# Attention with a learned distance bias, then a softplus feed-forward: round 1's scores moved into the bias stage, relus moved to ScalarE, rounds 0 and 1 reordered

## The chip, the core and the metric

The kernel runs on one core of one Trainium2 chip. The metric is the device time of one execution in microseconds (us). Three executions of the kernel before took 728.38, 728.56 and 729.88 us; their median is 728.56.

A core has five engines that run side by side and wait for one another on semaphores. TensorE (PE in the rows) does matmuls and transposes and writes to PSUM. VectorE (DVE) and ScalarE (ACT) do elementwise work on SBUF and PSUM. GpSimd (POOL) does elementwise work on SBUF, and SyncE (SP) issues DMAs. Each engine executes its own queue strictly in order.

## The reference

```
scores = (q @ k.T) / sqrt(D)                              B, H, S, D = 4, 8, 576, 64
x      = log1p(|i - j|) / log1p(max(i, 1))                for every pair of positions
bias   = relu(x * w1 + b1) @ w2                           32 hidden units, one output per head
attn   = softmax(scores + bias)
y      = attn @ v                                          -> (2304, 512)
h      = y @ w_in                                          512 -> 2048
out    = softplus(h) @ w_out                               2048 -> 512, float32
```

The bias depends on the position pair and the head, not on the batch.

## The kernel before, in words

**Bias stage.** 36 steps, one per 16 rows of positions. Step s needs four hidden tiles (relu of a scaled distance row plus a per-row term, `emit_hid`, 18 widths between 304 and 576 columns): the first three are always made by VectorE, the fourth by ScalarE for the steps in `RELU_ACT` and by VectorE for the others. TensorE contracts the 32 hidden units (`emit_mm`, into the PSUM tile `acc`, two banks, three buffers in the pool `pb`). `emit_rows` copies `acc` to the SBUF tile `e` in two pieces, nearly always on ScalarE (`EVAC_DVE` gives two of the 72 pieces to VectorE), and SyncE writes `e` to `e_d` in DRAM. The hidden tiles are made `LEAD` = 5 steps ahead of the copies. When 8 steps are written, later steps load bias tiles (128 by 576) back from `e_d`: tiles 0 and 5 after step 7, 1 and 6 after step 15, 2 and 7 after step 23. Tiles 3, 8 and 4 come last, and tile 4 needs the last step's rows.

**Splits.** q and k of a round are split into a high and a low part in fp32r (`u_split`), on VectorE in the bias stage for rounds 0 and 1 (`SPLITS` says at which steps), later with the low parts on GpSimd.

**Rounds.** 16 rounds, each one batch and one pair of heads, 9 score tiles of 128 rows. A score tile is four matmuls of 288 columns (eight for tile 4) into the PSUM tile `s`; VectorE then adds the bias and takes the row extreme in one custom instruction (`first` in `u_s`, written to the probabilities' tile `p` in SBUF); ScalarE takes the exponential in place (`second`); TensorE transposes `p`, VectorE or ScalarE copies the transposes from PSUM (`pt`), and TensorE multiplies with v (`o`). GpSimd copies small tails (`tl`).

**Order.** The order in which the queues are filled is written out by hand. In the strings `ROUND0`, `ROUND` and so on, a token names one piece of work: within round n, `Z`, `ZA`, `ZX` are matmuls, bias-and-extreme and exponential of a tile of round n itself, `S`, `A`, `X` the same for round n+1; `T` and `V` are transposes and their copy (`/a` on ScalarE, `/d` on VectorE); `P` the product with v; `Kh`, `Kl`, `Qh`, `Ql` the splits of round n+2; `I`, `R`, `C` the reciprocal sums; `O` the scaled output; `L`, `ZL` the tails. `SEQ0` puts five score tiles of round 0 into steps 21 to 31 of the bias stage, with one PSUM buffer for them (`ps_s`); a second one (`ps_s2`) is opened when the bias stage is over.

**After the rounds** comes the feed-forward part, which the change doesn't touch.

Of the kernel before, what the change touches and what calls it, by code (L numbers as in the profile page):

```python
# [24 lines left out]
EC = S + 15  # L25
# [63 lines left out]
LOADS0 = {8: "k", 14: "q", 44: "v1", 72: "v", 79: "w"}  # L89
# [15 lines left out]
def tile_log_bias_attention__then__softplus_ffn(  # L105
# [41 lines left out]
    ps_s = [pool(es_s, "ps_s", 1, "right", PSUM)]  # L147
# [15 lines left out]
    pb = pool(es_b, "pb", 3, space=PSUM)  # L163
# [185 lines left out]
    def u_s(n, t):  # L349
# [33 lines left out]

        def first():
# [23 lines left out]
        return pe, first, second  # L408
# [182 lines left out]

# [266 lines left out]
    for s in range(36):  # L858
# [18 lines left out]
    ps_s.append(pool(es_s, "ps_s2", 1, "right", PSUM))  # L877
# [73 lines left out]
    for n in range(N + 1):  # L951
# [9 lines left out]
        toks = {0: ROUND0, N - 1: ROUND15, N: ROUND16}.get(n, ROUND).split()  # L961
# [97 lines left out]
```

## Time and profile before

| | us |
|---|---|
| median of three runs | 728.56 |
| the profiled execution, its time | 728.94 |
| the profiled execution, span from first to last instruction | 727.1 |
| busy: PE, DVE, ACT, POOL | 695.6, 525.1, 524.8, 117.7 |
| share of the chain that ended last: PE, DVE, ACT, DMA | 87%, 5%, 3%, 2% |

The span is what the rows cover; the rest of the 728.94 lies around it. Busy time is summed over the whole span, so it hides that the engines' loads differ by stage. A row of the order-of-time view merges neighbouring instructions of one kind: its second number is the time from the first one's start to the last one's end, "x4" their count. Neighbours overlap a little, so the cost of one instruction in a full queue is the distance between starts, which is somewhat less than its duration.

### The profile page before, as it was taken

To read this page: it belongs to the slowest core of one execution; us is meant where nothing else is said; L and a number is where in the kernel's file an instruction comes from. 1 tells how busy PE (TensorE), PEld (TensorE's weight loads), DVE (VectorE), ACT (ScalarE), POOL (GpSimd) and SP (SyncE) were. 2 spreads that over 40 slices of the span, in tenths; PEclk is the share of its full clock that TensorE was granted. 3 is DMA by queue.
4 is the path that set the end of the run, shared out by engine and by line. 5 is a ranking of instruction groups with operands and counts; after the bars stand their busy time and mean duration, and the time that the engine had idled before them with its cause. 6 is when DMAs were issued, how large, how long until landed. Compare 5 with 4: busy or idle time off the path is not lost.

```text
span 727.1 us, 11884 instructions
## 1 busy us (share of the span) xinstructions
PE 695.6 (96%) x4160; PEld 547.1 (75%) x4160; DVE 525.1 (72%) x1109; ACT 524.8 (72%) x1060; POOL 117.7 (16%) x150
## 2 busy tenths in 40 slices
PE   4868999999999999989999999999999999999998
PEld 2224788877888778757888888988888888888886
DVE  7997877887888877667969595678685554656454
ACT  3967778888888887667867686777677665665654
POOL 0000446444554454120000000000000000000000
PEclk9989999999999999999999999999999999999999
DMA  4865686687677652654232030512020220312121
GB/s 135 316 200 207 219 290 208 212 250 241 191 211 218 186 169 81 166 160 160 75 140 93 30 112 4 175 63 83 30 73 15 102 72 1 130 44 81 65 76 41
DMA packets 47452, 96.77 MB, mean 133 GB/s; under 512 B 6928, under 2 KB 8352, under 8 KB 47392
## 3 DMA queue, kind: packets, MB, share of 16 engines
q1 hardware_dynamic: 47036, 95.41, 40.4%
q8 instruction: 33, 0.54, 0.3%
q10 hardware_dynamic: 356, 0.60, 0.3%
q14 instruction: 27, 0.22, 0.1%
HBM read 67.98 MB, written 28.01 MB: 132 GB/s over the span
## 4 chain that ended last, share of the span: by engine, by line
PE 87%; DVE 5%; ACT 3%; DMA 2%; issue 1%; POOL 1%; ACTq 0%; SPq 0%; POOLq 0%; DVEq 0%
PE y L826 28%; PE h L768 27%; PE s L376 11%; PE o L488 10%; PE t L447 8%; DVE m L202 3%; PE acc L215 2%; ACT p L403 1%; PE t L455 1%; DMA r_d<-r 1%; DMA e_d<-e 1%; DVE p L387 1%; ACT e L237 1%; DMA dist<-in_c_dist_dram 1%; ACT pt L341 0%
## 5 line engine op out<-in xcount | busy, mean ns | idle before, releaser
L768 PE MATMUL h<-x,wi 128*128 128x512 f32 (+1 forms) x960 | 216.4, 374 | 2.5 <-ACT wi L739 1.0
L826 PE MATMUL y<-wo,g 128*128 128x512 f32 x864 | 213.1, 394 | 0.0
L768 PEld LDWEIGHTS h<-x,wi 128*128 128x128 f32 x960 | 170.0, 189 | 39.7 <-ACT wi L739 1.4
L826 PEld LDWEIGHTS y<-wo,g 128*128 128x128 f32 x864 | 161.2, 188 | 37.1
L791 DVE SCALAR_TENSOR_TENSOR u<-u,e 128x512 f32<-128x512 f32 (+1 forms) x80 | 51.0, 637 | 110.0 <-ACT l L788 109.9
L376 PE MATMUL s<-kk,qq 128*128 128x288 f32 x640 | 118.2, 314 | 6.6 <-DVE m L387 6.4
L387 DVE CUSTOM_DVE_ANT_0 p<-s,b 128x576 f32<-128x576 f32 x144 | 106.0, 752 | 18.8 <-PE s L376 16.7
L403 ACT ACTIVATE p<-p,m 128x576 f32<-128x576 f32 x144 | 109.7, 765 | 4.1 <-DVE m L387 1.9
L784 ACT ACTIVATE e<-h 128x512 f32<-128x512 f32 (+1 forms) x80 | 44.3, 554 | 83.8 <-PE h L768 83.8
L376 PEld LDWEIGHTS s<-kk,qq 128*128 128x128 f32 x640 | 89.6, 189 | 12.6 <-DVE m L387 10.4
L447 PE MATMUL t<-ident,p 128*128 128x128 f32 x576 | 88.1, 275 | 2.3 <-ACT p L403 0.8
L341 ACT ACTIVATE pt<-t 128x384 f32<-128x384 f32 (+1 forms) x127 | 58.9, 488 | 41.9 <-PE t L447 39.1
L488 PE MATMUL o<-pt,vn 128*64 128x288 f32 (+3 forms) x672 | 84.5, 399 | 0.0
L447 PEld LDWEIGHTS t<-ident,p 128*128 128x128 f32 x576 | 65.8, 140 | 13.3 <-issue 7.0
L488 PEld LDWEIGHTS o<-pt,vn 128*64 128x64 f32 (+1 forms) x672 | 45.4, 136 | 32.5 <-issue 10.0
L798 ACT ACTIVATE g<-l 128x512 fp32r<-128x512 f32 (+1 forms) x80 | 46.8, 585 | 22.3 <-PE y L826 12.6
L343 DVE COPY pt<-t 128x384 f32<-128x384 f32 x97 | 50.3, 532 | 17.1 <-PE t L447 14.4
L215 PE MATMUL acc<-m,coef 128*32 128x512 f32 (+17 forms) x352 | 41.0, 547 | 15.6 <-DVE m L202 10.3
L420 POOL COPY tl<-p 128x128 f32<-128x128 f32 x80 | 26.0, 345 | 172.5 <-ACT p L403 171.5
L800 DVE TENSOR_TENSOR g<-l,g 128x512 fp32r<-128x512 f32 (+1 forms) x80 | 50.3, 629 | 3.8 <-ACT g L798 3.8
L795 DVE TENSOR_TENSOR l<-l,u 128x512 f32<-128x512 f32 (+1 forms) x80 | 50.4, 630 | 0.0
L793 DVE SCALAR_TENSOR_TENSOR l<-h,l 128x512 f32<-128x512 f32 (+1 forms) x80 | 50.4, 630 | 0.0
(55 smaller groups left out, 668.4 us busy)
## 6 DMA issues: line engine op xcount, KB each, us to landing
e_d<-e SPq DMA_DIRECT2D x36, 295.5 KB, 3.2
kn<-in_k_dram SPq DMA_DIRECT2D x16, 576.0 KB, 5.8
b<-e_d SPq DMA_DIRECT2D x32, 288.0 KB, 5.8
r<-in_moe_w_in_dram SPq DMA_DIRECT2D x16, 512.0 KB, 6.0
r<-in_moe_w_out_dram SPq DMA_DIRECT2D x16, 512.0 KB, 4.0
xr<-x_d SPq DMA_DIRECT2D x28, 256.0 KB, 3.4
vn<-in_v_dram SPq DMA_DIRECT2D x16, 320.0 KB, 3.5
qn<-in_q_dram SPq DMA_DIRECT2D x16, 288.0 KB, 5.2
```

Source lines behind the costliest of these rows:

```text
L215: nc.tensor.matmul(acc[32 * g:32 * g + 32, lo:hi], lhsT=coef.rearrange("p o h -> p (o h)"), rhs=hid[s, g][:, lo:hi], start=True, stop=True ...
L341: nc.scalar.activation(dst, src, AF.Copy)
L376: nc.tensor.matmul(ps[:, half, :SH], lhsT=qt[:, c0:c0 + 128], rhs=kt[:, hd, j, half * SH:half * SH + SH], start=(i == 0 and j == 0), stop= ...
L387: nc.vector.tensor_tensor_reduce(prob[n, t].rearrange("p (a c) -> p a c", a=2), st_["ps"][:, :, :SH], bias[pr, t].rearrange("p (a c) -> p ...
L403: nc.scalar.activation(p, p, AF.Exp, bias=st_["m"], scale=-1.0, accum_out=ssum[n][:, t:t + 1],)
L447: nc.tensor.transpose(ps[:, 128 * i:128 * i + 128], prob[n, t][:, 128 * jb:128 * jb + 128], ident,)
L488: nc.tensor.matmul(o[up, half, lo:hi], lhsT=v_n[n][rows, jb, hd], rhs=pt[n, jb][rows, c0:c0 + hi - lo], start=(jb == 0), stop=(jb == 4 and ...
L768: nc.tensor.matmul(ps[:, :nb], lhsT=wi[f][:, a, 128 * c:128 * c + 128], rhs=xs[bi, c][:, x_, :nb], start=(i == 0), stop=(i == 11),)
L791: nc.vector.scalar_tensor_tensor(u, u, -1.0, e, op0=ALU.add, op1=ALU.subtract)
L793: nc.vector.scalar_tensor_tensor(l, ps, 0.0, l, op0=ALU.max, op1=ALU.add)
L795: nc.vector.tensor_tensor(l, l, u, op=ALU.subtract)
L826: nc.tensor.matmul(y, lhsT=g[:, a, 128 * ts:128 * ts + 128], rhs=wo[f][:, w_], start=(first and i == 0), stop=(last and i == 2),)
```

## The change

Round 1's nine score tiles are computed during the bias stage. `raw` copies each from PSUM, without bias, into the place of its probabilities (`p`, SBUF); later `first` reads it there instead of in PSUM. The table `STAGE` replaces `SEQ0`: `21:D00` is round 0's tile 0 at step 21, as before with bias and exponential, and `21:R15` is round 1's tile 5, copied raw. The second PSUM buffer for scores exists from the start, and `acc` has two buffers instead of three. Round 1's split moves from step 12 to step 4. The fourth relu goes to ScalarE for steps 0 to 29 and 32 (31 relus, 22 before), and all 72 copies of `acc` go to ScalarE. `ROUND0` has no `S` tokens any more, and round 1 has an order of its own.

```diff
 ROUND0 = """
-Z7 S1 T20 ZA7 T30 V20/a A1 S6 S0 A6 T40 X1 ZX7 V30/a Z3 A0 V40/a S2 ZA3 A2 T00 Z8 S5 T10 ZX3
-ZA8 X0 ZX8 A5 ZL2 S7 V10/a S3 V00/d T12 T02 X6 V12/a A7 Z4 A3 V02/a ZA4 X7 T32 V32/d L1 ZX4 T22
-S4 I V22/a T01 R Qh1/d V01/a C S8 A4 X2 T11 X4 ZL3 T31 ZL4 P0 V11/d Kh/a Qh0/d L2 Ql0 L4 X5
-V31/d A8 Ql1 Kl X3 X8 L3 T21 V21/d T41 L0 P1 V41/d P2
+Z7 T20 T30 V20/a A1 ZA7 ZX7 V30/a A0 Z3 X1 T40 A6 X0 V40/a Z4 ZA3 A2 Z8 T10 T00 ZX3 ZA8 ZX8 A5
+V00/d ZL2 V10/a T12 T02 X6 V12/a A7 A3 V02/a ZA4 X7 T32 V32/d L1 ZX4 T22 V22/a I T01 R Qh1/d
+V01/a C A4 T11 X2 X4 ZL3 T31 ZL4 P0 Kh/a V11/d X5 Qh0/d L2 Ql0 Kl X3 A8 Ql1 L4 V31/d T21 L0 P1
+X8 L3 V21/d T41 V41/d P2
+"""
+
+ROUND1 = """
+Qh1/d Kh/a P3 P4 T20 Qh0/a I T02 S2 T11 V20/d V02/d V11/a A2 S3 T12 V12/a T00 V00/a S7 A3 O T10
...
 """
-LOADS0 = {8: "k", 14: "q", 44: "v1", 72: "v", 79: "w"}
+LOADS0 = {6: "k", 11: "q", 37: "v1", 63: "v", 70: "w"}
-RELU_ACT = {s for s in range(36) if s % 5 in (0, 2, 4)}
-
-EVAC_DVE = {3, 6}
-SPLITS = (2, 12)
+RELU_ACT = {*range(30), 32}
+
+SPLITS = (2, 4)
-SEQ0 = {21: 0, 24: 5, 26: 1, 29: 6, 31: 2}
+STAGE = """
+21:D00 21:R15 23:R10 24:R16 25:R12 26:D01 26:D05 30:R13 31:R11 31:R17 32:D02 33:D06 33:R18
+34:R14
+"""
-    ps_s = [pool(es_s, "ps_s", 1, "right", PSUM)]
+    ps_s = [pool(es_s, nm, 1, "right", PSUM) for nm in ("ps_s", "ps_s2")]
-    pb = pool(es_b, "pb", 3, space=PSUM)
+    pb = pool(es_b, "pb", 2, space=PSUM)
-        copy(e[:, 0:n], acc[:, 0:n][:, ::-1], 2 * s)
-        copy(e[:, n:EC], acc[:, 1:16 + i0], 2 * s + 1)
+        copy(e[:, 0:n], acc[:, 0:n][:, ::-1])
+        copy(e[:, n:EC], acc[:, 1:16 + i0])
+        def raw():
+            p = prob[n, t].rearrange("p (a c) -> p a c", a=2)
+            nc.scalar.activation(p, st_["ps"][:, :, :SH], AF.Copy)
+            st_["ps"] = p
+    def raw_(w, t):
+        unit = units["s", w, t] = u_s(w, t)
+        return [((1,), unit[0], unit[3])]
-        if s in SEQ0:
-            run(s_(0, SEQ0[s]))
-        else:
+        mine = [x.split(":")[1] for x in STAGE.split() if x.startswith(f"{s}:")]
+        for kind, w, t in mine:
+            run((s_ if kind == "D" else raw_)(int(w), int(t)))
+        if not mine:
             run([((), None)])
-    ps_s.append(pool(es_s, "ps_s2", 1, "right", PSUM))
-        toks = {0: ROUND0, N - 1: ROUND15, N: ROUND16}.get(n, ROUND).split()
+        toks = {0: ROUND0, 1: ROUND1, N - 1: ROUND15, N: ROUND16}.get(n, ROUND).split()
```

The queues show where the work now stands. First, TensorE's queue from step 22 of the bias stage on, before; `acc` rows are bias steps, an `s` row of x4 is one score tile, and `qq_121` and `qq_123` hold q of the even and the odd rounds:

```order
L215 MATMUL acc<-m,coef 32x368 x4
L376 MATMUL s<-kk,qq_121 128x288 x4
L215 MATMUL acc<-m,coef 32x384 x4
L215 MATMUL acc<-m,coef 32x400 x4
L215 MATMUL acc<-m,coef 32x416 x4
L376 MATMUL s<-kk,qq_121 128x288 x4
L215 MATMUL acc<-m,coef 32x432 x4
L215 MATMUL acc<-m,coef 32x448 x4
```

and the same place now (there the two are `qq_124` and `qq_126`):

```order
L224 MATMUL acc<-m,coef 32x368 x4
L382 MATMUL s<-kk,qq_124 128x288 x4
L382 MATMUL s<-kk,qq_126 128x288 x4
L224 MATMUL acc<-m,coef 32x384 x4
L224 MATMUL acc<-m,coef 32x400 x4
L382 MATMUL s<-kk,qq_126 128x288 x4
L224 MATMUL acc<-m,coef 32x416 x4
L382 MATMUL s<-kk,qq_126 128x288 x4
L224 MATMUL acc<-m,coef 32x432 x4
L382 MATMUL s<-kk,qq_126 128x288 x4
L224 MATMUL acc<-m,coef 32x448 x4
L382 MATMUL s<-kk,qq_124 128x288 x8
```

Where one score tile stood between two or three bias steps, one or two now stand between every two. Second, ScalarE's queue at steps 22 to 24, before (`m` rows are relus, `e` rows the copies of `acc`):

```order
L237 ACTIVATE e<-acc,tab 128x224
L237 ACTIVATE e<-acc,tab 128x367
L200 ACTIVATE m<-lw,pb_116 128x448
L237 ACTIVATE e<-acc,tab 128x208
L237 ACTIVATE e<-acc,tab 128x383
L237 ACTIVATE e<-acc,tab 128x192
L237 ACTIVATE e<-acc,tab 128x399
```

and now, with a relu in every step, a raw copy (`p<-s`) and an exponential (`p,ss_128`) among them:

```order
L245 ACTIVATE e<-acc,tab 128x224
L245 ACTIVATE e<-acc,tab 128x367
L209 ACTIVATE m<-lw,pb_119 128x448
L392 ACTIVATE p<-s 128x576
L245 ACTIVATE e<-acc,tab 128x208
L245 ACTIVATE e<-acc,tab 128x383
L209 ACTIVATE m<-lw,pb_119 128x464
L245 ACTIVATE e<-acc,tab 128x192
L245 ACTIVATE e<-acc,tab 128x399
L209 ACTIVATE m<-lw,pb_119 128x480
L414 ACTIVATE p,ss_128<-p,m 128x576
L392 ACTIVATE p<-s 128x576
```

Each copy pair of a step now has more work of ScalarE ahead of it. Third, GpSimd's queue at the end of round 0, before, with the low parts of round 2's q (`qq_121`, two halves) and k (`kk`):

```order
L324 TENSOR_TENSOR qq_121<-qn,qq_121 64x576
L420 COPY tl<-p_1051 128x128
L324 TENSOR_TENSOR qq_121<-qn,qq_121 64x576
L314 TENSOR_TENSOR kk<-kn,kk 128x2x576
L420 COPY tl<-p 128x128 x2
```

and now:

```order
L330 TENSOR_TENSOR qq_124<-qn,qq_124 64x576
L320 TENSOR_TENSOR kk<-kn,kk 128x2x576
L330 TENSOR_TENSOR qq_124<-qn,qq_124 64x576
L431 COPY tl<-p_903 128x128
L431 COPY tl<-p 128x128 x2
```

The low part of k moved from third to second place among the three subtractions.

## Rows read from the trace of the kernel before

**Rows 1.** Busy time in stretches of 20 us, by engine (instructions); header row first.

```profile
core 0: us, PE busy (x) PEld busy (x) DVE busy (x) ACT busy (x) POOL busy (x), PEclk, DMA share, GB/s
...
60.00:80.00 20.00, 18.13 (x154) 12.87 (x145) 12.98 (x35) 15.15 (x38) 1.42 (x5) 0.93 0.63 204
...
120.00:140.00 20.00, 20.00 (x165) 17.09 (x162) 16.06 (x40) 15.89 (x37) 11.80 (x11) 1.00 0.64 203
```

**Rows 2.** VectorE's instruction groups, 6.18 to 66.6 us: busy us, mean ns, idle before.

```profile
L202 DVE TENSOR_SCALAR m<-lw,pb 128x560 f32<-128x560 f32 (+17 forms) x122 | 44.7, 438 | 0.1
```

**Rows 3.** ScalarE's instruction groups, 6.18 to 68 us.

```profile
L237 ACT ACTIVATE e<-acc,tab 128x576 f32<-128x576 f32 (+34 forms) x70 | 31.3, 519 | 16.2 <-issue 6.2 <-DVE e L239 4.6 <-PE acc L215 2.1
```

**Rows 4.** ScalarE in order of time: start us, us, instruction, [idle before it].

```profile
21.47 1.72 ACT L237 ACTIVATE e<-acc,tab 128x480 f32<-128x480 f32 x4
23.02 0.66 ACT L200 ACTIVATE m<-lw,pb 128x384 f32<-128x384 f32 x1
23.53 0.95 ACT L237 ACTIVATE e<-acc,tab 128x448 f32<-128x448 f32 x2
...
66.29 1.70 ACT L237 ACTIVATE e<-acc,tab 128x32 f32<-128x32 f32 x4
...
70.31 0.76 ACT L403 ACTIVATE p<-p,m 128x576 f32<-128x576 f32 x1
...
71.07 0.75 ACT L341 ACTIVATE pt<-t 128x384 f32<-128x384 f32 x2
```

**Rows 5.** SyncE's DMA issues in order of time.

```profile
72.28 0.53 SPq L297 DMA_DIRECT2D b<-e_d  x1
```

**Rows 6.** VectorE in order of time, round 0.

```profile
77.60 0.76 DVE L387 CUSTOM_DVE_ANT_0 p<-s,b 128x576 f32<-128x576 f32 x1 [0.88 <-ACT pt L341]
...
80.75 0.46 DVE L343 CAST qq<-qn 64x576 fp32r<-64x576 f32 x1 [0.85 <-DMA qn<-in_q_dram]
...
84.93 1.73 DVE L343 CAST qq<-qn 64x576 fp32r<-64x576 f32 x1
```

**Rows 7.** GpSimd in order of time, end of round 0.

```profile
84.92 1.42 POOL L324 TENSOR_TENSOR qq<-qn,qq 64x576 fp32r<-64x576 f32 x1
86.42 2.73 POOL L314 TENSOR_TENSOR kk<-kn,kk 128x1152 fp32r<-128x1152 f32 x1
```

**Rows 8.** TensorE in order of time.

```profile
42.99 2.22 PE L215 MATMUL acc<-m,coef 128*32 128x384 f32 x24
...
63.49 3.04 PE L215 MATMUL acc<-m,coef 128*32 128x512 f32 x48
...
69.21 1.31 PE L376 MATMUL s<-kk,qq 128*128 128x288 f32 x8
...
88.71 1.15 PE L376 MATMUL s<-kk,qq 128*128 128x288 f32 x4
```

**Rows 9.** VectorE in order of time, bias stage.

```profile
6.18 8.26 DVE L202 TENSOR_SCALAR m<-lw,pb 128x576 f32<-128x576 f32 x20
14.37 0.23 DVE L239 TENSOR_SCALAR e<-acc,tab 128x31 f32<-128x31 f32 x1
...
17.83 0.75 DVE L239 TENSOR_SCALAR e<-acc,tab 128x528 f32<-128x528 f32 x1
...
23.32 5.55 DVE L202 TENSOR_SCALAR m<-lw,pb 128x400 f32<-128x400 f32 x17
28.80 0.93 DVE L343 CAST qq<-qn 64x576 fp32r<-64x576 f32 x2
...
35.55 1.54 DVE L324 TENSOR_TENSOR qq<-qn,qq 64x576 fp32r<-64x576 f32 x2
...
38.40 5.67 DVE L202 TENSOR_SCALAR m<-lw,pb 128x352 f32<-128x352 f32 x17
```

**Rows 10.** The page's groups: two SBUF inputs (L795), one in PSUM (L793).

```profile
L795 DVE TENSOR_TENSOR l<-l,u 128x512 f32<-128x512 f32 (+1 forms) x80 | 50.4, 630 | 0.0
L793 DVE SCALAR_TENSOR_TENSOR l<-h,l 128x512 f32<-128x512 f32 (+1 forms) x80 | 50.4, 630 | 0.0
```

More of the change, by code (lines that the diff above doesn't have):

```diff
@@ L52 @@
 ROUND0 = """
-Z7 S1 T20 ZA7 T30 V20/a A1 S6 S0 A6 T40 X1 ZX7 V30/a Z3 A0 V40/a S2 ZA3 A2 T00 Z8 S5 T10 ZX3
-ZA8 X0 ZX8 A5 ZL2 S7 V10/a S3 V00/d T12 T02 X6 V12/a A7 Z4 A3 V02/a ZA4 X7 T32 V32/d L1 ZX4 T22
-S4 I V22/a T01 R Qh1/d V01/a C S8 A4 X2 T11 X4 ZL3 T31 ZL4 P0 V11/d Kh/a Qh0/d L2 Ql0 L4 X5
-V31/d A8 Ql1 Kl X3 X8 L3 T21 V21/d T41 L0 P1 V41/d P2
+Z7 T20 T30 V20/a A1 ZA7 ZX7 V30/a A0 Z3 X1 T40 A6 X0 V40/a Z4 ZA3 A2 Z8 T10 T00 ZX3 ZA8 ZX8 A5
[5 more added lines that the diff above has]
+Qh1/d Kh/a P3 P4 T20 Qh0/a I T02 S2 T11 V20/d V02/d V11/a A2 S3 T12 V12/a T00 V00/a S7 A3 O T10
+R Ql1 X3 C V10/a S4 Kl S0 T41 T22 B0 A7 V41/a A4 B1 S1 V22/a A0 Ql0 T30 T01 V30/a V01/a S6 X7 A1
+X4 S5 B2 A6 T21 X2 V21/d T31 V31/d S8 A8 B3 T32 X0 A5 X5 X1 T40 X8 P0 L2 X6 L0 P1 V40/d L3 B4 L4
+P2 L1 V32/d
 """
@@ L233, in emit_rows, with copy @@
         r = rho[:, s:s + 1]
-        def copy(dst, src, on):
-            if on not in EVAC_DVE:
-                nc.scalar.activation(dst, src, AF.Copy, scale=r)
-            else:
-                nc.vector.tensor_scalar(dst, src, r, None, op0=ALU.mult)
-        copy(e[:, 0:n], acc[:, 0:n][:, ::-1], 2 * s)
-        copy(e[:, n:EC], acc[:, 1:16 + i0], 2 * s + 1)
+        def copy(dst, src):
+            nc.scalar.activation(dst, src, AF.Copy, scale=r)
+        copy(e[:, 0:n], acc[:, 0:n][:, ::-1])
+        copy(e[:, n:EC], acc[:, 1:16 + i0])
         nc.sync.dma_start(
@@ L406, in second @@
             )
-        return pe, first, second
+        return pe, first, second, raw
     def tail(n, i):
@@ L579, in s_ @@
     def s_(w, t):
-        pe, first, second = u_s(w, t)
+        pe, first, second, _ = u_s(w, t)
         def last():
@@ L868, in tile_log_bias_attention__then__softplus_ffn @@
             emit_bias(0, t)
-        if s in SEQ0:
-            run(s_(0, SEQ0[s]))
-        else:
+        mine = [x.split(":")[1] for x in STAGE.split() if x.startswith(f"{s}:")]
+        for kind, w, t in mine:
+            run((s_ if kind == "D" else raw_)(int(w), int(t)))
+        if not mine:
             run([((), None)])
```

## The prediction, made before the changed kernel was run

> **What bounds the kernel now.** I read four views, in this order.
>
> First the busy time by stretch [rows 1]. From 120 us on TensorE is busy 20.00 of every 20 us, and the other engines have slack; there the kernel is bound by the number of matmuls, which the change leaves as it is. Between 60 and 80 us TensorE reaches 18.13. What can be won lies ahead of the point from which TensorE runs without a gap.
>
> Then the groups of the bias stage. VectorE is the bound there: its 122 relus leave 0.1 us idle ahead of them [rows 2], while the copies on ScalarE sum up 16.2 us of idle time before them [rows 3]. In ScalarE's order of time the last pair of copies ends at 66.29 + 1.70 = 67.99 us [rows 4]. That is the end of the bias stage.
>
> Then the wait that follows it. SyncE can issue the load of bias tile 4 only when the last rows are in DRAM, at 72.28 [rows 5]; VectorE takes up tile 4 of round 0 at 77.60 [rows 6], ScalarE its exponential at 78.40 (last piece of the same chain), and the rest of round 0 hangs on that. The q of round 2 is loaded behind it; VectorE waits 0.85 us for it and casts it at 80.75 [rows 6]. GpSimd then does two subtractions of 1.42 us for q and one of 2.73 us for k, which ends at 86.42 + 2.73 = 89.15 [rows 7]. TensorE's first score tile of round 2 starts at 88.71, takes 1.15 us instead of the usual 0.65 because of that, and ends at 89.86 [rows 8]. From there TensorE is full. So 67.99 to 89.86 is mostly a chain of latencies, and what counts is when the last pair of copies ends.
>
> **Part 1: the bias stage.** Prices first, as distances between starts. A pair of copies on ScalarE costs (23.02 − 21.47)/2 = 0.78 us, a relu of 384 columns 23.53 − 23.02 = 0.51, an exponential 71.07 − 70.31 = 0.76 [rows 4]. The mean of the 31 relus is 424 columns; I take 0.54. The raw copy (576 columns out of PSUM) isn't in the trace. Below it is the copy of 384 columns out of PSUM at 0.75/2 = 0.38 [rows 4], above it the exponential of 576 columns at 0.76; nothing makes it cheaper than the former, which has fewer columns. I take 0.55, nearer to the plain copy, whose operation it is. On TensorE a bias step of 384 to 416 columns costs 2.22/3 = 0.74, one of the last three 3.04/3 = 1.01, a score tile 1.31/2 = 0.65 [rows 8].
>
> *VectorE.* It is full from 6.18 on and reaches the end of step 22's relus at 38.40 plus 7 of 17 relus in 5.58 us, at 40.7 [rows 9]. Ahead of this the change takes away nine fourth relus (steps 1, 3, 6, 8, 11, 13, 16, 18, 21) at about 0.36, between 8.19/20 = 0.41 for wide ones and 5.48/17 = 0.32 for narrow ones, so 3.2 us; and two copies, 0.23 and 0.75 less overlaps, 0.84. It adds round 1's casts of q, which came later before, 28.80 to 29.77, 0.97 [rows 9]. That gives 40.7 − 3.2 − 0.84 + 0.97 = 37.6. Step 23's three relus follow (38.6), then the low parts of round 1's q at 1.57 (40.2) [rows 9].
>
> *TensorE* meets two waits here. Round 1's tile 5 stands right behind step 22 and needs that low part, so it waits until 40.2, and behind it the matmuls of steps 23 and 24 wait. Then round 1's tile 0 needs the PSUM buffer of round 0's tile 0, which VectorE frees after nine more relus (3.2) and its bias-and-extreme, 0.76 less the overlap [rows 6], 0.7: 44.1. From there TensorE has 11 score tiles (7.2) and 11 bias steps (25 to 35, from 0.77 to 1.01, 10.0) up to the last one: 44.1 + 17.2 = 61.3.
>
> *ScalarE* from 44.1 has 11 pairs (8.6), two relus (1.1), eight raw copies (4.4) and three exponentials (2.3), 16.4 us, and would end at 60.5. *VectorE* from 44.1 has 32 relus at 0.41 or less (13.1) and two more bias-and-extremes (1.4) up to its last relu, so 58.6 at the latest.
>
> TensorE is last. Two engines with 17.2 and 16.4 us of work that hand every tile to each other through two PSUM buffers each can't both be full; I add 0.8 us for one tile that each waits for, and the last pair, 0.78: the bias stage ends at 62.9, that is **5.1 us earlier**. The bounds: no such loss gives 62.1 (5.9 earlier). If every one of the eight raw copies stalls TensorE by its own 0.55, 66.5 (1.5 earlier).
>
> **Part 2: round 0.** The latencies from the last copy to tile 4 of round 0 stay as they are, so everything behind them moves by those 5.1 us. TensorE loses nine tiles here, ten units of 0.65, 6.5 us; most of that lay beside the chain. On it there was one such tile behind the reciprocal sums, about 0.5. The subtraction for k moves ahead of the second one for q, up to 1.42 earlier [rows 7], but the products with v that stand ahead of round 2's first tile on TensorE then end later than it. I take **0.6** for both together, between 0 and 1.9.
>
> The bias-and-extreme of round 1's nine tiles now reads two operands from SBUF instead of one from PSUM. That costs nothing by itself: the page's two-operand groups take 630 ns with both inputs in SBUF and 630 ns with one in PSUM [rows 10]. ScalarE's content in round 0 (13 exponentials, 8 transposes' copies, one k) is the same as before. SyncE's bias tile 3 now stands one write earlier in its queue and waits there for the rows of step 31, with three writes of `e` behind it; those rows are copied some six pairs of work before the last pair, which covers it; without that cover the price is one write's latency, the 4.3 us from 67.99 to 72.28 [rows 4, 5].
>
> **Part 3: rounds 1 to 15 and the feed-forward part.** No instruction is added or taken away, and TensorE is full: 0.
>
> Sum: −5.1 − 0.6 = −5.7. The profiled execution took 728.94 with a span of 727.1, so I expect a span of about 721.4 and 723.2 for such an execution; the median of the runs is 0.4 lower, so **722.9 us**.
>
> **The rivals.**
>
> *Slower: ScalarE becomes the bound of the bias stage.* By the prices above ScalarE gets nine relus (4.9), eight raw copies (4.4), two more copies (0.8), and one exponential fewer before the last pair (−0.8): 9.3 us. If its 16.2 us of waits [rows 3] stay, all but the 4.6 us that it waited for VectorE's copy of `acc`, the bias stage ends 9.3 − 4.6 = 4.7 later, and the kernel takes 733.3. The point is where ScalarE still waits for more than 16.2 − 9.3 = 6.9 us. For it: two `acc` buffers instead of three, and in-order queues. Against it: most of those waits were for a VectorE that had no slack, and it is that engine which is relieved. The Trainium skill, ScalarE: Activation LUTs, section "Rules for kernel authors", speaks for this rival: it gives relu to VectorE rather than to ScalarE. By that rule the move of the relus alone would be a loss. The trace agrees on the prices: 0.51 us for 384 columns on ScalarE [rows 4], 0.32 to 0.41 on VectorE [rows 9]. Chance 0.08.
>
> *Given back: the hand-overs cost as much as the work saved.* This is the upper bound of part 1, 66.5, with nothing won in round 0: 727.1. Chance 0.10.
>
> *A block between VectorE and GpSimd.* In the trace a cast of 64 by 576 takes 0.46 us alone at 80.75, but 1.73 at 84.93 [rows 6], for as long as GpSimd's subtraction of 84.92 to 86.34 [rows 7]. Round 1's last bias-and-extreme stands right behind the cast after which GpSimd starts its subtractions; if it is blocked too, it waits 1.42 to 2.73 us, with the copies of three transposes and the products with v behind it. That gives 722.9 + 1.4 to 2.7, some 725. The Trainium skill, SBUF — State Buffer, section "Who interferes with whom", says just this: a VectorE instruction with two SBUF inputs and a GpSimd instruction that reads SBUF exclude each other for the whole instruction, and the instruction before, with its score in PSUM, does not fall under it. No run shows it yet for this instruction. Against it: VectorE issues first here, and GpSimd would wait for 0.7 instead. Chance 0.13.
>
> *More: TensorE was the bound of round 0 as well.* Then much of the 6.5 us comes on top of a part of the 5.1, and the time is about 719.5. Against it stands the chain of latencies above. Chance 0.12.
>
> **How the numbers follow.** My forecast has 0.57, the rivals 0.08, 0.10, 0.13 and 0.12. The likeliest gives 722.9. The range takes in the bounds of parts 1 and 2, the block and the larger gain: 718.5 to 727.0. What is left out is the slower rival, most of what is given back, and a little below. About 0.2%, some 1.5 us, is what a measurement of this kernel can tell from no change. Faster by more: 0.57 + 0.12 + 0.13 and a part of the second rival, 0.85; within it 0.07; slower 0.08.
>
> **What would show it.** In the profile after: ScalarE's last copy pair ends near 62.9; TensorE has no gap of over 2 us behind 44 us; the raw copies cost about 0.55 each; tile 4 of round 0 comes 9.6 us after the last pair, as before; the first score tile of round 2 ends near 84.2; from 120 us on TensorE is busy 20.00 of 20. I am wrong if the last pair ends after 66, if TensorE shows gaps in round 1, or if the bias-and-extreme of round 1 takes over 1 us.

## The result, and the profile after the change

The changed kernel takes **722.38 us** (median of 6 runs, 721.72 to 723.40) against 728.47 us for the kernel before in the same session (727.19 to 729.88). The ratio is 0.9915, with a 95% interval of 0.990 to 0.993: faster by 6.1 us. The prediction said 722.9, within 718.5 to 727.0. The total was right; several of its terms were not, and one part of the change turned out to cost time.

The profiled execution took 723.4 us with a span of 721.6, 5.5 less than the 727.1 before. First its busy time by stretch: the stretch in us, its length, then per engine the busy time with the number of instructions, the granted clock of TensorE, the share and rate of the DMA.

```profile
core 0: us, PE busy (x) PEld busy (x) DVE busy (x) ACT busy (x) POOL busy (x), PEclk, DMA share, GB/s
40.00:60.00 20.00, 17.67 (x150) 8.47 (x147) 18.79 (x49) 18.71 (x43) 2.46 (x1) 1.00 0.68 243
60.00:80.00 20.00, 17.63 (x116) 11.72 (x114) 14.05 (x38) 17.25 (x43) 3.04 (x7) 0.84 0.75 252
80.00:100.00 20.00, 20.00 (x158) 15.30 (x158) 15.77 (x34) 14.86 (x36) 12.64 (x13) 0.99 0.70 222
120.00:140.00 20.00, 20.00 (x165) 17.41 (x165) 16.19 (x44) 16.86 (x40) 10.66 (x12) 1.00 0.59 176
```

From 120 us on TensorE is full, as before [rows 1]. The stretch from 60 to 80 has a granted clock of 0.84, which a finer view explains below.

Next the groups of the bias stage, 6 to 65 us, of VectorE and of ScalarE: busy us, mean ns of one, idle time ahead of them and what ended it.

```profile
L211 DVE TENSOR_SCALAR m<-lw,pb 128x576 f32<-128x576 f32 (+17 forms) x113 | 41.7, 444 | 0.1
...
L245 ACT ACTIVATE e<-acc,tab 128x576 f32<-128x576 f32 (+35 forms) x72 | 33.3, 532 | 4.9 <-DMA e_d<-e 1.9 <-PE acc L224 1.5 <-ACT e L245 0.9
L209 ACT ACTIVATE m<-lw,pb 128x528 f32<-128x528 f32 (+17 forms) x31 | 20.7, 680 | 4.5 <-DVE pb L188 4.5
L392 ACT ACTIVATE p<-s 128x576 f32<-128x576 f32 x8 | 5.4, 673 | 0.3 <-PE s L382 0.3
```

VectorE has 113 relus instead of 122 [rows 2] and still no idle time ahead of them. ScalarE's copies now have 4.9 us of idle time ahead of them instead of 16.2 [rows 3]. The L392 group is new: the raw copies of round 1's scores. Eight of the nine moved tiles lie ahead of the last pair, tile 4 behind it.

In ScalarE's order of time the bias stage ends at 64.03 + 0.91 = **64.94 us**, 3.05 earlier than the 67.99 of [rows 4]:

```profile
42.24 0.73 ACT L392 ACTIVATE p<-s 128x576 f32<-128x576 f32 x1
42.77 0.99 ACT L245 ACTIVATE e<-acc,tab 128x208 f32<-128x208 f32 x2
...
64.03 0.91 ACT L245 ACTIVATE e<-acc,tab 128x16 f32<-128x16 f32 x2 [0.53 <-PE acc L224]
```

A raw copy costs ScalarE 42.77 − 42.24 = 0.53 us of its queue. The last pair waits 0.53 us for TensorE, whose order of time is this:

```profile
40.02 1.69 PE L382 MATMUL s<-kk,qq 128*128 128x288 f32 x8
41.64 1.52 PE L224 MATMUL acc<-m,coef 128*32 128x384 f32 x16
44.81 0.79 PE L382 MATMUL s<-kk,qq 128*128 128x288 f32 x4 [1.65 <-DVE m L398]
45.54 0.91 PE L224 MATMUL acc<-m,coef 128*32 128x416 f32 x8
46.37 0.79 PE L382 MATMUL s<-kk,qq 128*128 128x288 f32 x4
47.10 0.93 PE L224 MATMUL acc<-m,coef 128*32 128x432 f32 x8
...
50.56 0.79 PE L382 MATMUL s<-kk,qq 128*128 128x288 f32 x4 [0.19 <-ACT p L392]
51.28 1.79 PE L224 MATMUL acc<-m,coef 128*32 128x464 f32 x16
53.42 1.90 PE L224 MATMUL acc<-m,coef 128*32 128x496 f32 x16 [0.35 <-ACT e L245]
...
62.73 1.18 PE L224 MATMUL acc<-m,coef 128*32 128x512 f32 x16
...
77.99 2.19 PE L499 MATMUL o<-pt,vn 128*64 128x288 f32 x8
...
86.08 0.78 PE L382 MATMUL s<-kk,qq 128*128 128x288 f32 x4
```

From 44.81 to 62.73 + 1.18 = 63.91 TensorE waits for only 0.19 and 0.35 us. A score tile between bias steps costs 47.10 − 46.37 = 0.73 us there. The first score tile of round 2 ends at 86.86, 3.0 earlier than the 89.86 of [rows 8].

Behind the last pair, SyncE, VectorE and GpSimd in order of time:

```profile
69.10 0.52 SPq L303 DMA_DIRECT2D b<-e_d  x1
```

```profile
72.80 0.76 DVE L398 CUSTOM_DVE_ANT_0 p<-s,b 128x576 f32<-128x576 f32 x1
...
76.36 0.46 DVE L349 CAST qq<-qn 64x576 fp32r<-64x576 f32 x1 [0.53 <-DMA qn<-in_q_dram]
...
78.35 0.74 DVE L398 CUSTOM_DVE_ANT_0 p<-p,b 128x576 f32<-128x576 f32 x1
...
83.81 1.27 DVE L536 TENSOR_SCALAR ss<-ss 128x9 f32<-128x9 f32 x1
```

```profile
78.29 0.96 POOL L431 COPY tl<-p 128x128 f32<-128x128 f32 x1 [2.74 <-ACT p L414]
79.34 1.41 POOL L330 TENSOR_TENSOR qq<-qn,qq 64x576 fp32r<-64x576 f32 x1
80.83 2.64 POOL L320 TENSOR_TENSOR kk<-kn,kk 128x1152 fp32r<-128x1152 f32 x1
83.54 1.51 POOL L330 TENSOR_TENSOR qq<-qn,qq 64x576 fp32r<-64x576 f32 x1
```

Tile 4 is taken up at 72.80, 7.86 us behind the last pair; before it was 77.60 − 67.99 = 9.61 [rows 4, 6]. The load of its bias isn't what differs. From the load's issue to the landing of its second half, which the trace marks, it takes 3.58 us before (72.28 to 75.86) and 3.54 after (69.10 to 72.64). But before, tile 4's scores (eight matmuls) were on TensorE only from 76.16 to 77.46, later than its bias was there; the new order of round 0 makes them among the twelve at 67.67. TensorE before and after:

```profile
76.16 1.30 PE L376 MATMUL s<-kk,qq 128*128 128x288 f32 x8
```

```profile
67.67 1.83 PE L382 MATMUL s<-kk,qq 128*128 128x288 f32 x12
```

The bias-and-extreme that reads its score from SBUF (p<-p,b) takes 0.74, no longer than the one from PSUM.

The finer view by stretches shows TensorE at half clock in round 0:

```profile
72.00:74.00 2.00, 1.36 (x7) 0.95 (x7) 1.56 (x6) 2.00 (x6) 0.53 (x2) 0.86 0.93 324
74.00:76.00 2.00, 1.95 (x9) 1.01 (x7) 1.05 (x3) 1.60 (x6) 0.29 (x1) 0.50 0.98 320
```

With nine tiles fewer in its queue TensorE waited more in 70 to 74 (busy 1.01 and 1.36 of 2 us, before 1.89 and 2.00); its granted clock fell to 0.50, the 1.2 GHz level, and stayed there until 80 us. So the eight products with v at 77.99 took 2.19 us.

The chain of work that ended last, in order of time, shows what the last pair leads to. From 64.03 to 73.31 it runs through ScalarE's queue without a gap, and from 73.36 to the first score tile of round 2, but for one copy by ScalarE at 75.97, through TensorE's:

```profile
72.17 0.75 ACT p L414 x2
72.92 0.39 ACT pt L347
73.31 0.04 issue
73.36 1.52 PE t L458 x6
```

The load of tile 4 isn't on it.

Where the 5.5 us came from follows from four marks. The last pair is 3.05 us earlier. From it to round 2's products with v (the first run of 42, at 115.14 before and 111.14 after) it takes 47.15 before and 46.20 after, 0.95 less. From there to the first output matmul of the feed-forward part (332.48 and 327.05) it takes 217.34 and 215.91, 1.43 less. The rest is the same within 0.05.

### The profile page after: what moved, and what is told of

Same layout as the page of the kernel before. It is cut to its first block, busy times and chain, and to the rows that moved or that the text cites. A ratio compares the mean times of both kernels' runs of the same rounds, so it can differ in the third digit from the quotient of the medians.

```text
span 721.6 us, 11904 instructions
## 1 busy us (share of the span) xinstructions
PE 692.5 (96%) x4160; PEld 543.8 (75%) x4160; DVE 519.9 (72%) x1098; ACT 533.5 (74%) x1080; POOL 120.2 (17%) x150
## 4 chain that ended last, share of the span: by engine, by line
PE 92%; ACT 4%; DVE 3%; DMA 1%; issue 1%; SPq 0%; ACTq 0%; DVEq 0%
PE y L841 28%; PE h L783 27%; PE o L499 12%; PE s L382 11%; PE t L458 9%; PE acc L224 4%; PE t L466 1%; DVE m L211 1%; ACT e L245 1%; ACT p L414 1%; DMA dist<-in_c_dist_dram 1%; ACT pt L347 1%; DVE qq L330 0%; DVE x L773 0%; PE t L550 0%
## 5 line engine op out<-in xcount | busy, mean ns | idle before, releaser
L398 DVE CUSTOM_DVE_ANT_0 p<-s,b 128x576 f32<-128x576 f32 x135 | 99.5, 752 | 17.2 <-PE s L382 16.7
L458 PE MATMUL t<-ident,p 128*128 128x128 f32 x576 | 89.7, 280 | 3.2 <-ACT pt L347 1.7
L349 DVE COPY pt<-t 128x384 f32<-128x384 f32 (+1 forms) x97 | 50.6, 534 | 21.2 <-PE t L458 17.3
L813 ACT ACTIVATE g<-l 128x512 fp32r<-128x512 f32 (+1 forms) x80 | 46.8, 586 | 21.8 <-PE y L841 12.2
L431 POOL COPY tl<-p 128x128 f32<-128x128 f32 x80 | 28.5, 377 | 165.3 <-ACT p L414 161.8
L224 PE MATMUL acc<-m,coef 128*32 128x512 f32 (+17 forms) x352 | 35.9, 502 | 17.1 <-DVE m L211 8.8
```

Source lines behind the costliest of these rows:

```text
L224: nc.tensor.matmul(acc[32 * g:32 * g + 32, lo:hi], lhsT=coef.rearrange("p o h -> p (o h)"), rhs=hid[s, g][:, lo:hi], start=True, stop=True ...
L349: nc.vector.tensor_copy(dst, src)
L398: nc.vector.tensor_tensor_reduce(prob[n, t].rearrange("p (a c) -> p a c", a=2), st_["ps"][:, :, :SH], bias[pr, t].rearrange("p (a c) -> p ...
L458: nc.tensor.transpose(ps[:, 128 * i:128 * i + 128], prob[n, t][:, 128 * jb:128 * jb + 128], ident,)
```

## The experiments

Every run has an interval for its ratio against the kernel before on the same chip. "P run" is the start of the 42 products with v in round 2, after which TensorE is full. The relus are those on ScalarE, the buffers those for scores and for the bias steps during the bias rows, the tiles those of round 1 computed there. The marks in us are those of one profiled execution each. The kernel after, profiled twice (after, e11), has its last pair at 64.94 and 64.20, so a difference of less than some 0.7 us between two rows may be chance.

| run | relus | buffers | tiles | last pair ends | P run | between | ratio [95%] |
|---|---|---|---|---|---|---|---|
| before | 22 | 1 + 3 | 0 | 67.99 | 115.14 | 47.15 | 1 |
| after | 31 | 2 + 2 | 9 | 64.94 | 111.14 | 46.20 | 0.9915 [0.990, 0.993] |
| e1 | 22 | 2 + 2 | 9 | 69.69 | 115.22 | 45.53 | 0.9995 [0.9984, 1.0007] |
| e2 | 31 | 1 + 3 | 0 | 66.32 | 112.57 | 46.25 | 0.9946 [0.9934, 0.9958] |
| e3 | 31 | 2 + 2 | 9 | 64.50 | 110.89 | 46.39 | 0.9923 [0.9910, 0.9936] |
| e4 | 31 | 2 + 2 | 7 | 64.01 | 109.98 | 45.97 | 0.9917 [0.9903, 0.9931] |
| e5 | 31 | 2 + 2 | 9 | 64.56 | 109.84 | 45.28 | 0.9923 [0.9906, 0.9939] |
| e6 | 31 | 2 + 2 | 0 | 61.40 | 107.51 | 46.11 | 0.9889 [0.9871, 0.9906] |
| e7 | 31 | 2 + 2 | 9 | 67.62 | 113.19 | 45.57 | 0.9962 [0.9947, 0.9977] |
| e8 | 31 | 2 + 2 | 9 | 66.90 | 113.16 | 46.26 | 0.9992 [0.9979, 1.0006] |
| e9 | 22 | 2 + 2 | 0 | 70.58 | 117.49 | 46.91 | 1.0014 [1.0002, 1.0025] |
| e10 | 33 | 2 + 2 | 0 | 60.86 | 107.31 | 46.45 | 0.9889 [0.9870, 0.9908] |
| e11 | as after | | | 64.20 | 110.27 | 46.07 | 0.9922 [0.9906, 0.9938] |
| e12 | as e6 | | | 61.53 | 107.81 | 46.28 | 0.9884 [0.9866, 0.9902] |

**e1: the relus alone undone.**

```diff
-RELU_ACT = {*range(30), 32}
+RELU_ACT = {s for s in range(36) if s % 5 in (0, 2, 4)}
```

> The change with its 31 relus on ScalarE put back to the 22 of before; all else as changed. Theory A (the gain is the earlier end of the bias stage, and that comes from relieving VectorE): VectorE reaches step 22 about 3 us later, the last pair of copies ends near 67.9 us instead of 64.94, and the kernel takes about 725.4. Theory B (the gain comes from the score tiles taken out of round 0, TensorE being its bound): the time stays at 722.4, since no tile moves.

Measured 729.07 us against 729.29, no difference; neither theory had that. Nine tiles fewer in round 0 gave no time on the whole: the stretch behind the last pair did get shorter, by 1.6 us, but the bias stage ended 1.7 us later than before, at 69.69.

**e2: the relus alone done**, in the kernel before, with its two VectorE copies given to ScalarE.

```diff
-RELU_ACT = {s for s in range(36) if s % 5 in (0, 2, 4)}
-EVAC_DVE = {3, 6}
+RELU_ACT = {*range(30), 32}
+EVAC_DVE = set()
```

> The kernel before with the 31 relus and all copies of acc on ScalarE, and nothing else of the change. Theory A: VectorE is done with its last relu 3.8 us earlier, near 58.2 instead of 62.0, the last pair ends near 64.2 instead of 67.99, and the kernel takes about 724.7. Theory B: no tile leaves round 0, so 728.5, as before.

Measured 725.10 against 729.29, near theory A's 724.7; the last pair is 1.67 earlier, not 3.8. The relus alone bring 0.54 of the 0.85%. What then stops TensorE is in its groups, 6 to 62 us:

```profile
L376 PE MATMUL s<-kk,qq 128*128 128x288 f32 x20 | 5.1, 387 | 6.2 <-DVE m L387 6.1
```

Ahead of its score tiles TensorE waits 6.1 us for VectorE's bias-and-extreme, which frees the one score buffer and stands behind three to twelve relus in VectorE's queue. Behind the longest of these waits the granted clock fell (0.73 in 60 to 62, 0.50 in 62 to 64), and the last three bias steps took 4.72 us instead of 3.04 [rows 8]:

```profile
59.84 0.80 PE L376 MATMUL s<-kk,qq 128*128 128x288 f32 x4 [3.02 <-DVE m L387]
60.57 4.72 PE L215 MATMUL acc<-m,coef 128*32 128x512 f32 x48
```

**e3: is it the half clock of round 0?** The transposes of four groups are made three times, with the same result, to keep TensorE busy there (`TWICE` names them).

```diff
-                for i, t in enumerate(need):
+                for i, t in list(enumerate(need)) * (3 if (n, jb, c) in TWICE else 1):
```

> The change, with the transposes of four groups of round 0 (column blocks 0 and 1, row groups 0 and 2) issued three times over into the same place, so that TensorE has work in its gaps between 69 and 74 us; the result is the same. Theory C (the half clock of 73 to 80 us, which followed those gaps, costs about 3 us): the granted clock stays at 1.00 there, the products with v take their 1.19 us per 8 instead of 2.19, and the kernel takes about 719.4. Rival (ScalarE, full from 64.8 to 75 us, sets the pace of round 0, the clock only uses up slack): the clock stays up and the time stays at 722.4; or the 24 transposes themselves cost up to 2 us and it takes 724.

Measured 723.26. The clock is 1.00 throughout 60 to 96, and the eight products with v have their usual duration:

```profile
77.89 1.19 PE L500 MATMUL o<-pt,vn 128*64 128x288 f32 x8
```

The time is as after; theory C's 719.4 did not come. Holding the clock up with added work gains nothing net. What the half clock costs by itself this run doesn't tell, since the 24 added transposes take time too.

**e4: two of the nine tiles (8 and 4) left in round 0**, with the places of three loads moved by two tokens.

```diff
-21:D00 21:R15 23:R10 24:R16 25:R12 26:D01 26:D05 30:R13 31:R11 31:R17 32:D02 33:D06 33:R18
-34:R14
+21:D00 21:R15 23:R10 24:R16 25:R12 26:D01 26:D05 30:R13 31:R11 31:R17 32:D02 33:D06
...
-Z7 T20 T30 V20/a A1 ZA7 ZX7 V30/a A0 Z3 X1 T40 A6 X0 V40/a Z4 ZA3 A2 Z8 T10 T00 ZX3 ZA8 ZX8 A5
-V00/d ZL2 V10/a T12 T02 X6 V12/a A7 A3 V02/a ZA4 X7 T32 V32/d L1 ZX4 T22 V22/a I T01 R Qh1/d
+Z7 T20 T30 V20/a A1 ZA7 ZX7 V30/a A0 Z3 X1 T40 A6 X0 V40/a Z8 ZA3 A2 T10 T00 S8 Z4 ZX3 ZA8 ZX8 A5 A8
+V00/d ZL2 V10/a T12 T02 S4 X6 V12/a A7 A3 V02/a ZA4 X7 T32 V32/d L1 ZX4 T22 V22/a I T01 R Qh1/d
...
```

> The change, with round 1's tiles 8 and 4 left in round 0, as score tiles straight into bias-and-extreme (no raw copy), placed in TensorE's gaps after the transposes of block 0. Theory A with C: the last pair ends about 0.9 us earlier (64.0), ScalarE has two raw copies less (1.06 us) before round 0, TensorE's gaps are filled with three units of 0.73 us and the clock stays up: about 719.5. Theory B (each tile left in round 0 costs its TensorE time): 722.4 + 2.2, so 724.6.

Measured 723.13, the same as after, so neither theory's time. The last pair is 0.93 earlier and the P run 1.16. In the profiled execution one later round took 15.51 instead of 15.23 us, and the feed-forward part had a stretch of half clock, so its span is not shorter than that of after (722.3 against 721.6).

**e5: the new order of round 1 undone**, so that it runs in the general order.

```diff
-toks = {0: ROUND0, 1: ROUND1, N - 1: ROUND15, N: ROUND16}
+toks = {0: ROUND0, N - 1: ROUND15, N: ROUND16}
```

> The change whole, but round 1 runs in the general order of the rounds again. Theory A (what stands behind the last copy pair moves with it; round 1's order is only adapted to which tiles are ready): the stretch from the last copy pair to the first run of round 2 stays at about 46.2 us, as in the kernel after (46.20) and in the run with the relus alone, which has the general order (46.25); time as after, within 0.7 us of ratio 0.9915. Rival B (the new order of round 1 brought part of the gain): the stretch goes back to the 47.15 us of the kernel before, and the ratio to about 0.993 or more.

Measured 722.88, as after; the stretch behind the last pair did not grow (45.28). Round 1's new order isn't where the gain comes from.

**e6: relus and second score buffer, no tile moved.** It is e2 with this:

```diff
-    ps_s = [pool(es_s, "ps_s", 1, "right", PSUM)]
+    ps_s = [pool(es_s, nm, 1, "right", PSUM) for nm in ("ps_s", "ps_s2")]
-    pb = pool(es_b, "pb", 3, space=PSUM)
+    pb = pool(es_b, "pb", 2, space=PSUM)
-    ps_s.append(pool(es_s, "ps_s2", 1, "right", PSUM))
```

> The kernel before with the relus and copies on ScalarE, and with two PSUM buffers for scores and two for the bias steps during the bias rows instead of one and three; no tile of round 1 is moved. It separates the second score buffer from the moved tiles. Theory A1 (with 31 relus on ScalarE TensorE is the bound and it is the wait for the one score buffer that keeps the last copy pair at 66.32 with the relus alone; the moved tiles cost TensorE up to 8 x 0.73 = 5.8 us in the bias rows): the last pair ends before the 64.94 us of the kernel after, between 62 and 64, and the time is 720 to 722. Rival A2 (five score tiles meet that wait too seldom for the buffer to matter, and what the moved tiles bring lies behind the bias rows): the last pair stays at 66 to 67 and the time at the 725 of the run with the relus alone.

Measured **720.65**, 2.2 us less than e5 on the same chip: better than the kernel after. The last pair ends at 61.40, a little earlier even than theory A1 had it. The groups of TensorE, 6 to 62 us, beside that of e2:

```profile
L215 PE MATMUL acc<-m,coef 128*32 128x512 f32 (+17 forms) x352 | 37.8, 511 | 17.8 <-ACT e L237 10.9 <-DVE m L202 6.8
L376 PE MATMUL s<-kk,qq 128*128 128x288 f32 x28 | 5.8, 340 | 0.0
```

The 6.1 us of waits ahead of the score tiles are gone, and the last pair comes 66.32 − 61.40 = 4.92 us earlier than in e2. Of these, 4.72 − 3.04 = 1.68 are the half clock at the end of e2's bias stage, which followed a wait for the one buffer. So in the kernel after, the second score buffer helps, and the moved tiles, with the earlier split and the orders that go with them, take 64.94 − 61.40 = 3.54 us of it away again.

**e7: raw copies on VectorE**, those of the even tiles: four of the eight ahead of the last pair, and tile 4's behind it.

```diff
-            nc.scalar.activation(p, st_["ps"][:, :, :SH], AF.Copy)
+            if n == 1 and t % 2 == 0:
+                nc.vector.tensor_copy(p, st_["ps"][:, :, :SH])
+            else:
+                nc.scalar.activation(p, st_["ps"][:, :, :SH], AF.Copy)
```

> The kernel after with four of the eight raw copies (round 1's tiles 0, 2, 6 and 8) on VectorE instead of ScalarE. Theory T (TensorE is the bound of the bias rows from 44.8 us on: 11 score tiles at 0.73 and 11 bias steps): the last copy pair stays at 64.9 within 0.4, the time as after. Rival S (ScalarE sets the pace through the hand-overs): 4 x 0.53 = 2.1 us less on ScalarE, last pair near 62.9, ratio 0.9887. Second rival (the copies stand behind relus in VectorE's queue and free the score buffers later): last pair 1 us or more later than 64.9, ratio 0.993 or more.

Measured 725.81, 2.9 more than e5 on the same chip; the last pair is 2.68 later than in after. The second rival holds. In the groups of TensorE, 6 to 68 us, the score tiles wait for those copies (L393):

```profile
L382 PE MATMUL s<-kk,qq 128*128 128x288 f32 x63 | 11.8, 316 | 5.4 <-DVE p L393 2.8 <-DVE m L401 1.7 <-DVE qq L330 0.9
```

**e8: every raw copy made twice.**

```diff
             nc.scalar.activation(p, st_["ps"][:, :, :SH], AF.Copy)
+            nc.scalar.activation(p, st_["ps"][:, :, :SH], AF.Copy)
```

> The kernel after with each of the eight raw copies made twice on ScalarE. Theory T (TensorE is the bound; ScalarE had 19.1 - 16.4 = 2.7 us of slack from 44.8 us on): the 8 x 0.53 = 4.2 us eat that slack and add about 1.5 us, so the last pair ends near 66.4 and the ratio is 0.9935. Rival S (ScalarE sets the pace): the full 4.2 us, last pair near 69.2, ratio 0.997 or more. If the copies were covered altogether: 64.9 and no change.

The two readings disagree. In the profiled execution the last pair is 1.96 later, near theory T's 1.5 and far from the 4.2 of the rival. TensorE now waits for ScalarE ahead of single tiles, as in this row of its order of time:

```profile
51.86 0.79 PE L382 MATMUL s<-kk,qq 128*128 128x288 f32 x4 [1.22 <-ACT p L393]
```

But the median is 727.64, 4.8 above that of e5 on the same chip, as the rival had it. The profiled execution (727.41) has 4.0 more span than that of after: 2.0 up to the P run, 0.3 between the P runs of rounds 3 and 4, 1.5 in a stretch of half clock in the feed-forward part. So in that execution about half of the doubled copies was absorbed. The second copy also frees the score buffer later, as the row shows, so this run doesn't measure ScalarE's slack alone. Where the rest of the 4.8 lies in the other runs is open.

**e9: the buffers alone**, the edit of e6 in the kernel before.

> The kernel before with two PSUM buffers for scores and two for the bias steps during the bias rows; relus and tiles as before. Theory U (the buffer is worth something only once VectorE no longer is the bound; before, VectorE's relus leave no idle time and set the end): last copy pair within 0.7 us of 67.99, ratio between 0.998 and 1.002. Rival I (the buffer's gain is independent of the relus; it was 725.1 against 720.65, 0.57% with them): last pair near 63, ratio 0.994. Third case (one buffer less for the bias steps hurts): ratio over 1.002.

Measured 729.67, 0.14% slower than before (interval 1.0002 to 1.0025), within theory U's ratio, though the profiled last pair is 2.6 later, not within 0.7. Without the relus on ScalarE, TensorE still waits for a VectorE that is behind, here for 3.74 us. The granted clock fell behind that wait (0.50 from 62 to 68), and the last three bias steps took 5.13 us instead of 3.04 [rows 8], which is 2.1 of the 2.6:

```profile
63.16 1.33 PE L376 MATMUL s<-kk,qq 128*128 128x288 f32 x4 [3.74 <-DVE m L387]
64.42 5.13 PE L215 MATMUL acc<-m,coef 128*32 128x512 f32 x48
```

The buffer is worth something only together with the relus; the two gains aren't independent. (e1 adds the tiles to e9 and has the two VectorE copies on ScalarE; in its profile the clock is 1.00 throughout the bias stage. The intervals of the two ratios overlap.)

**e10: e6 with two more relus on ScalarE.**

```diff
-RELU_ACT = {*range(30), 32}
+RELU_ACT = {*range(31), 32, 34}
```

> The run with relus and two score buffers (last copy pair 61.40, 720.65 us) with two more relus, those of steps 30 and 34, on ScalarE. Theory V (late in the bias rows VectorE is again the one that is full, and ScalarE has 2.6 us of waits for its bias-and-extreme): VectorE's last relus end 2 x 0.43 = 0.9 us earlier and the last pair by 0.3 to 0.9; ratio 0.988 to 0.989. Rival W (TensorE is full from 54.9 to 62 by its last six bias steps and two tiles): last pair unchanged within 0.3, the ratio 0.989. Against both: relus on ScalarE hold up its copies, last pair later than 61.8, ratio over 0.990.

The last pair ends at 60.86, 0.54 earlier than in e6 and 0.67 earlier than in e12, as theory V had it, though that is no more than the kernel after differs from itself; the time, 720.95, can't be told from that of e6. The P run is only 0.2 earlier.

**e11 and e12: the kernel after and e6 again, on one chip.**

> The kernel after, once more on the same chip as the next run, so that the two can be compared directly: ratio 0.9915 as before; first run of round 2's products with v (o, 42 matmuls in a row) at 111.1 with a granted clock of 0.50 in part of round 0, or near 110 without.

> The run with relus and two score buffers once more beside the kernel after. Theory M (the moved tiles cost more in the bias rows than they give back in round 0): about 1.8 us faster than the kernel after on the same chip, ratio to the kernel before 0.989. Rival N (the two differ by their chips and by the clock in single executions alone): both ratios within 0.001 of each other.

Measured 723.27 (722.05 to 725.25, 6 runs) and 720.68 (720.14 to 721.56, 4 runs): the two don't overlap, and e6 is 2.6 us faster. Theory M holds. Their last pairs, from ScalarE's order of time, first e11, then e12:

```profile
63.29 0.91 ACT L245 ACTIVATE e<-acc,tab 128x16 f32<-128x16 f32 x2 [0.54 <-PE acc L224]
```

```profile
59.85 1.68 ACT L237 ACTIVATE e<-acc,tab 128x32 f32<-128x32 f32 x4
```

## Why the prediction was right, and where it was not

**The bound.** Right. In all fourteen profiled executions the stretch from the last pair to the P run is 45.3 to 47.2 us, while the last pair itself moves from 60.86 to 70.58. What sets the time is mostly when the bias stage ends; e8, whose time grew by more than its last pair moved, is the exception that stays open.

**Part 1, the size.** Forecast 62.9, measured 64.94; 2.0 of the 5.1 us did not come. The step that failed is TensorE's sum: "11 score tiles (7.2) and 11 bias steps", started at 44.1, with 0.8 for waits. The start came at 44.81 (+0.7), because VectorE was done with the low part of q at 39.31 + 1.54 = 40.85 and not at 40.2:

```profile
39.31 1.54 DVE L330 TENSOR_TENSOR qq<-qn,qq 64x576 fp32r<-64x576 f32 x2
```

The 11 tiles cost 8.0, since one costs 0.73 between bias steps; 0.65 was taken from two tiles in a row [rows 8]. The 11 bias steps cost 10.6 instead of 10.0, and the waits 0.54 instead of 0.8. So it took 19.1 instead of 18.0, and the last pair ended 1.03 behind that instead of 0.78. The order of the engines was right: TensorE was last. The wait for the low part of q, forecast until 40.2, doesn't show in this profile, where TensorE is on earlier bias steps and a tile of round 0 until then; in e11 it is 1.01 us, until 40.62.

**Part 1, the raw copy.** Taken as 0.55, measured 0.53. The choice of the nearer row was right.

**Part 1, what it didn't separate.** Its sum held the eight tiles ahead of the last pair at 5.2 us on TensorE's path (8 × 0.65), and part 2 their return at no more than 1.9. By these two numbers the tiles cost more than they give, which the prediction did not say. e6 against after shows it: 3.54 us in the bias stage, and nothing returned (46.11 against 46.20). Where round 0 kept its clock (e1, e5, e7: 45.28 to 45.57) some 0.5 to 0.8 was returned. Of 8 × 0.73 = 5.8 only 3.5 appears, and e10 suggests that in e6 VectorE's relus, which end at 58.23, are the next limit. Nor is all of the 3.54 TensorE's time for tiles: 45.54 − 43.47 = 2.07 are there at step 25 already, behind only two of them, when TensorE in the kernel after waits 1.65 us for a VectorE that did round 1's low parts first. In e6 that step is:

```profile
43.47 0.91 PE L215 MATMUL acc<-m,coef 128*32 128x416 f32 x8 [0.49 <-ACT e L237]
```

No run moves the split by itself, so its share of the price is open. The prediction did not price the second score buffer by itself; e2 and e6 show that the buffer, once the relus are on ScalarE, is worth as much again as the relus alone (0.57% behind 0.54%; at the last pair of single profiles 4.92 us behind 1.67).

**Part 2.** "The latencies from the last copy to tile 4 stay as they are" was wrong: 7.86 instead of 9.61 us. The latency of the load did stay (3.58 and 3.54 us). The step that failed is reading the stretch from 67.99 to 77.60 as a chain through that load: before, tile 4's bias landed at 75.86, and the tile was taken up only when TensorE had made its scores, at 77.46. The new order of round 0 makes them earlier, which the prediction did not price. Nor did those 1.75 us shorten the whole, as the chain that ended last doesn't pass tile 4's load after the change. The first score tile of round 2 ends 21.9 us behind the last pair in both kernels.

On that chain TensorE ran at half clock and took 1.0 us more for the first eight products with v alone. The half clock was not foreseen. In the five profiles with moved tiles whose clock held in round 0 (e1, e3, e4, e5, e7) that score tile ends 20.0 to 21.2 us behind the last pair, in the three where it fell (after, e8, e11) 21.8 to 22.0. At the P run it is 45.28 to 45.57 us (e1, e5, e7; e3 and e4 have more work for TensorE there) against 46.07 to 46.26. So the half clock costs some 0.5 to 1.0 us by then, an estimate from profiles that differ in other ways too.

The forecast of 0.6, between 0 and 1.9, is missed by the kernel after at that score tile and met at the P run, with 0.95. But its reasons aren't shown: e2 and e6, which move no tile and keep round 0's order, are 0.90 and 1.04 us shorter there than the kernel before. Why they are is open.

**Part 3.** Forecast 0. The rounds from 2 on agree to 0.12 us (182.63 and 182.75 from the P run of round 2 to that of round 14). The 1.43 us in the feed-forward part are a stretch of half clock behind the same two waits for weights (1.00 and 0.76 us). Ten matmuls, before and after:

```profile
328.50 4.14 PE L768 MATMUL h<-x,wi 128*128 128x512 f32 x10 [0.76 <-DVE wi L741]
```

```profile
324.62 2.58 PE L783 MATMUL h<-x,wi 128*128 128x512 f32 x10 [0.76 <-DVE wi L756]
```

Of the fourteen profiled executions six had it (before, e4, e6, e8, e9, e12), with 217.3 to 217.7 us from the P run to the first output matmul, and eight did not, with 215.8 to 216.0. It comes and goes in kernels with the same code there, and e6 is the faster one with it. So this part of the 5.5 us isn't shown to be the change's. It made up in this pair of profiles for what part 1 lacked: the closeness of 722.9 to 722.4 is partly luck.

**The rivals.** *ScalarE as the bound* did not come: its point was 6.9 us of remaining waits, and 4.9 remained. The Trainium skill's rule in ScalarE: Activation LUTs, "Rules for kernel authors", to give relu to VectorE, would have made the relus' move a loss; e2 measures a gain of 0.54%, because VectorE had no idle time and ScalarE 16.2 us. e7 points the same way: copies given to VectorE cost 2.9 us, through the buffer that they free later. *The block* of the bias-and-extreme did not come either: it took its usual 0.74 at 78.35, and GpSimd's copy of 78.29 beside it took 0.96 instead of 0.30. VectorE's cast of 77.98 to 78.42 was running when that copy began, so the rows don't tell which of the two instructions held it up. But another instruction of VectorE was blocked: an addition for the reciprocal sums on 128 by 9 elements took 1.27 us at 83.81, until GpSimd's subtraction of 83.54 to 85.05 was over. The next one, at 100.57, takes 0.17. This is not new with the change: before, the same addition took 2.49 us at 86.69. The Trainium skill, SBUF — State Buffer, "Who interferes with whom", states that a tensor_scalar can contend with GpSimd for a shared port if its operands meet certain conditions, and that whoever issues first then holds the port for the whole instruction. The 1.27 us agree; whether this addition meets the conditions no trace here shows. *Given back* and *more* did not come, though *more* had a part of its mechanism right: tile 4 did wait for TensorE before.

## What to carry to other kernels

When an edit has several parts, price each by what it adds ahead of the point that sets the end and by what it returns behind it, and drop the part whose return is smaller, even if the sum is a gain: here, on one chip, the relus and a second buffer gave 1.16% (e12), and with the moved tiles 0.78% were left (e11). A buffer that nobody seems to lack, because another engine is the bound, can be the next thing that is lacking: e9 gave nothing with it, e6 another 0.57% behind e2's 0.54%. Filling an engine's idle time with work from later is only free if that work doesn't stand in the queue that decides when the stage ends.

## What was not expected of the hardware

TensorE's granted clock fell to 0.50 in round 0 after stretches with 1.01 and 1.36 us busy of 2 (and in e11 after 1.30 and 1.41), though the engine had been at 1.00 for all the bias stage; before, it had been at 0.50 within the bias stage, in 40 to 42, 50 to 52 and 60 to 62, and at 1.00 in round 0. Nor does the queue alone decide it: e5 has the same one there, was busy 1.30, 1.33 and 1.17 us of 2 in 70 to 76, and stayed at 1.00 in round 0. Keeping it up with added work was possible (e3) and gained nothing net. At the end of the bias stage, where TensorE's work comes last, it cost more: the last three steps took 1.7 us longer in e2 and 2.1 in e9.

A VectorE instruction on 9 columns can take over 2 us: in e6 the addition for the reciprocal sums, started behind GpSimd's subtraction for k, which ran from 79.50 to 82.13, ended only with it, at 82.16.

```profile
79.77 2.39 DVE L525 TENSOR_SCALAR ss<-ss 128x9 f32<-128x9 f32 x1 [1.63 <-ACT p L403]
```

Whether another place for it, away from GpSimd's subtractions, would save time wasn't tried.
